# Walking the first softplus stage in tile pairs over two token blocks, with halves in the stage after it

## The chip, the cores and the metric

The kernel runs on one core of a Trainium2 chip. Time is the device time of one execution in microseconds (us). Three runs of the kernel before took 735.72, 737.89 and 739.29 us, so their median is 737.89 us. The engines of the core are called PE (TensorE, matrix products), PEld (its weight loads), DVE (VectorE), ACT (ScalarE), POOL (GpSimd) and SP (SyncE, which issues nearly all DMAs). Each of them works through its own list of instructions in a fixed order.

## The reference, cut to what matters

```python
def reference(**kw):
    attn = _attn_ref(q, k, v, a_re, a_im)        # a decaying linear attention, 2 batches x 8 heads x 768 steps x 48
    x = attn.transpose(0, 2, 1, 3).reshape(1536, 384)
    x = _moe_ref(x, w_in, w_out)                  # h = x @ w_in;  softplus(h) @ w_out;  d_ff = 2048
    return _moe2_ref(x, domain_probs, w1, w2)     # sum over 4 experts: p_e * (relu(x @ w1_e) @ w2_e);  F = 1024

def softplus(h):
    return np.maximum(h, 0.0) + np.log1p(np.exp(-np.abs(h)))
```

The attention state decays by a complex factor per step, `a_re + i a_im`, whose magnitude is capped at 0.999. `w_in` and `w_out` arrive as 64-bit numbers.

## The kernel before, in words

The 1536 tokens are two batches of 768. Attention goes through twelve chunks of 128 tokens in six groups `n` of two chunks (`c` is 0 or 1). The dense part is cut into twelve stages `k` (`ORDER` sets their order). Stages 0 and 1 are the two halves of the 2048 softplus columns for the first batch, 2 to 5 are its four experts, 6 to 11 are the same for the second batch. A stage has eight tiles `f` of 128 columns. Stage 0 goes over its batch in three blocks of 256 tokens, each of which needs the output of one attention group (block 0 needs group 0, and so on); the later stages take two blocks of 384 tokens.

One step (`step`, for a `k`, a block and an `f`) issues the first product `h` (`gemm1`, nine products on PE) and the softplus on ACT (abs, exp, ln) and DVE (tile `e`), then for the step before it the split of the result into a high and a low part `g` (`second`), and for the step three back (`LAG`) the second product `y` (`third`, nine products that add up in PSUM over the tiles `f`). In stage 0 two tiles `f` share one bank and one softplus. When all eight tiles are added, `third` empties PSUM: stage 0 copies to `Y`, stage 1 adds `Y`, splits the sum and writes it over `X`, which the experts read.

Weights of stages 0 and 1 are joined from two 32-bit words into a 32-bit float by three DVE instructions on each half (`join`, lines 70 to 72; tiles `fA`, `fB`), split in a high part on ACT (line 181) and a low part on DVE (line 182), and written to a scratch in memory for the second batch. `A` tiles hold `w_in`, `B` tiles hold `w_out`; there are four pairs per stage. They go round a ring of `NR` = 9 slots. Three weight tiles of stage 1 (n = 2, 3, 4) are put into a pool of their own, `early`, which `swap` later gives up for `X` of the second batch.

For attention, `back(n)` turns a chunk's q and k (`tp`, PE, copied out by ACT), takes scores (`sp`), masks them on DVE (tile `A` on line 684), mixes (`yps`), adds the state (`sps`, then `S` on DVE) and writes `X` (hi by ACT on line 721, lo by DVE on line 722). `logmag`, `s2_units` and `trig` make the decay and the angles: `prefix` sums along a chunk (`pf`, `pl`), and the last row of one chunk is carried into the next through a DMA and an addition on POOL (`carry`, lines 617 to 619, and line 574). An `excursion` loads the other table of ACT's functions (line 97) and loads the first again after it.

The program is recorded unit by unit: `put` and `events` give each unit a due time on a scale where a step is 1, stage 0 begins at 0, and stage 1 at 24. A scheduler behind the recording then sets the order in which each engine's instructions stand.

Of the kernel before, what the change touches and what calls it, by code (L numbers as in the profile page):

```python
# [75 lines left out]
def fast_path(ctx: ExitStack, tc, bad, wsc, qkv, a_re, a_im, w_in, w_out, probs, w1, w2, out):  # L76
# [9 lines left out]
    psum = ctx.enter_context(tc.tile_pool(name="psum", bufs=1, space=PSUM))  # L86
    early_ctx = ExitStack()
    early = early_ctx.enter_context(tc.tile_pool(name="early", bufs=1, side="right"))

# [3 lines left out]
    def behind(ins, earlier):  # L93
        tc.add_manual_dep(ins.ins, earlier.ins.name, NOSYNC, reason="order on one engine")
# [108 lines left out]

    XB = [xa.tile([P, 2, KT, S], F32R, name="X0"), None]
    Yt = [None]
    acc = {}
    home = [ac, None]
    ps_y = [None]
    h_pair = [None]
# [81 lines left out]
    def third(k, blk, f):  # L291
        s = k % 6
        g = g_t.pop((k, blk, f))
        wt = W[k, f // 2 * 2 + 1]
        nf = HALF if k in FAST else FH
        opens, closes = f % nf == 0, f % nf == nf - 1
        b, c0, nch, tok, TB = span(k, blk)
        nj, width = (KT, TB) if s < 2 else (nch, DM)
        if opens:
            yt = psum.tile([P, 2, 512], F32, tag="y", name=f"y{k}_{blk}_{f}", bufs=1)  # L300
            if k == 0:
                ps_y[0] = [yt[:, j // 2, j % 2 * 256:j % 2 * 256 + 256] for j in range(nj)]
            else:
                zt = psum.tile([P, 512], F32, tag="z", name=f"z{k}_{blk}_{f}", bufs=1)
                ps_y[0] = [yt[:, 0, :width], yt[:, 1, :width], zt[:, :width]]
        ys = ps_y[0]
        for j in range(nj):
            for n, (p, q) in enumerate(((0, 0), (0, 1), (1, 0))):
                if s < 2:
                    l_, r_ = wt[:, q, f % 2, j * P:(j + 1) * P], g[p] if k == 0 else g[:, p, :]  # L310
                else:
                    l_, r_ = g[:, p, j * P:(j + 1) * P], wt[:, q, f % 2, :]
                mate = k == 0 and j == 1
                mm = nc.tensor.matmul(ys[j], l_, r_, start=(opens and n == 0 and not mate),  # L314
                                      stop=(closes and n == 2), skip_group_check=k == 0)
                if opens and n == 0:
                    if mate:
                        behind(mm, opened)
                    opened = mm
        if not closes:  # L320
# [6 lines left out]
        elif s == 1:  # L327
            for j in range(KT):
                u = Yt[0][:, j, tok]
                hi, lo = (XB[b][:, i, j, tok] for i in range(2))  # L330
                nc.vector.tensor_tensor(u, ys[j], u, ALU.add)
                nc.scalar.copy(hi, u)
                nc.vector.tensor_tensor(lo, u, hi.bitcast(F32), ALU.subtract)
# [472 lines left out]

    def spare(shape, dt, nm):
        return early.tile(shape, dt, tag=nm, name=nm)

    def lag_out(k):  # L810
        return lambda: (second(*pipe[-1]) if pipe else None)

    for m, k in enumerate(ORDER):
        if k in FAST:
# [23 lines left out]
            continue  # L838
        blks = 3 if k == 0 else 2
        put([lambda k=k, blk=blk, f=f: step(k, blk, f) for blk in range(blks) for f in range(FH)], base[m], base[m + 1])  # L840
        for n in range(8):
            if k == 0:
                pos, gap = -5.2 + 1.6 * n, 0.4
            elif k == 1:
                pos, gap = 8.3 + 2.3 * n, 0.6
            else:
                pos, gap = base[m - 1] + 1 + 1.7 * n, 1.5
            in_early = k == 1 and n in (2, 3, 4)
            if not in_early:
                if len(ring) >= NR:  # L850
                    pos = max(pos, ring[len(ring) - NR] + 0.1)
                ring.append(base[m + 1] - FH + 2 * (n // 2) + 1 + (LAG if n % 2 else 0))
            for i, u in enumerate(weights(k, n, spare if in_early else slot)):
                events.append((pos + gap * i, len(events), u))
    for pos, need, last, k, n in sorted(fast_events):
# [8 lines left out]
    put([lambda: logmag(1, both)] + s2_units(1) + [lambda: s1_load(2), lambda: squares(2, both), lambda: ratio(2, both)]  # L864
        + [excursion(lambda: trig(1), lambda: arctan(2))], -8, 0)
    put(back(1), -0.7, 6.3)
    put([lambda: logmag(2, both)] + s2_units(2) + [excursion(lambda: trig(2))], 1.3, 7.5)
    put(back(2), 8.3, 15.7)

    def swap():  # L870
        early_ctx.close()
        xb = ctx.enter_context(tc.tile_pool(name="xb", bufs=1, side="right"))
        XB[1] = xb.tile([P, 2, KT, S], F32R, name="X1")

    put([swap], base[2] + 3.5, base[2] + 4)
    put([load_probs], base[2] + 1, base[2] + 2)
# [286 lines left out]
```

## Time and profile before

| | |
|---|---|
| median of three runs | 737.89 us (735.72 to 739.29) |
| the profiled execution: span from first to last instruction | 736.2 us |
| PE busy | 703.0 us (95%) |
| DVE busy | 584.7 us (79%) |
| ACT busy | 487.0 us (66%) |
| mean granted TensorE clock | 0.986 of full |

The page gives the span of the profiled execution and not its own device time; the span lies between the fastest run and the median. The strip below cuts the span into 40 slices of 18.4 us, each digit being a busy share in tenths. PE is nearly always busy from the third slice on, DVE is full from the second to the eighth and then eases, and the granted clock is low in the second slice.

```
PE   1688999999999999999999999999999999999996
DVE  6999999955875854648888779988788899988963
ACT  7887886878896856345686666555556667666640
PEclk9699999999999999999999999999999999999998
```

### The profile page before, as it was taken

How to read it: one execution, taken by the hardware profiler on the slowest of the kernel's cores; microseconds unless marked ns; L12 is line 12 of the kernel's file. 1: busy time of each engine (PE TensorE's matmuls, PEld its weight loads, DVE VectorE, ACT ScalarE, POOL GpSimd, SP SyncE). 2: the span in 40 equal slices, each digit the busy share in tenths (PEclk: the TensorE clock that was granted, in tenths of full speed). 3: DMA queues.
4: the chain of work that ended last, by engine and by line, in shares of the span. 5: the costliest groups of instructions: out<-in, count | busy, mean ns of one | idle time of the engine just before them, and what ended most of it. 6: DMA issues, size and time to landing. Idle time of an engine off the chain costs nothing.

```text
span 736.2 us, 13313 instructions
## 1 busy us (share of the span) xinstructions
PE 703.0 (95%) x5171; PEld 676.2 (92%) x5171; DVE 584.7 (79%) x1150; ACT 487.0 (66%) x898; POOL 33.3 (5%) x31
## 2 busy tenths in 40 slices
PE   1688999999999999999999999999999999999996
PEld 0477899999899999999999999999999999999996
DVE  6999999955875854648888779988788899988963
ACT  7887886878896856345686666555556667666640
POOL 1132010000111011000000000000000000000000
PEclk9699999999999999999999999999999999999998
DMA  7655666721211420121022130213454445554501
GB/s 264 195 175 170 230 190 195 228 84 44 75 55 59 122 81 2 59 86 44 23 86 65 29 102 21 87 44 98 128 159 146 137 151 172 151 172 140 172 32 69
DMA packets 36486, 83.56 MB, mean 113 GB/s; under 512 B 4544, under 2 KB 13376, under 8 KB 36416
## 3 DMA queue, kind: packets, MB, share of 16 engines
q1 hardware_dynamic: 36128, 82.35, 35.5%
q8 instruction: 42, 0.69, 0.4%
q10 hardware_dynamic: 288, 0.30, 0.1%
q14 instruction: 28, 0.23, 0.1%
HBM read 73.95 MB, written 8.65 MB: 112 GB/s over the span
## 4 chain that ended last, share of the span: by engine, by line
PE 70%; DVE 10%; DMA 9%; ACT 8%; issue 2%; POOL 1%; SPq 0%; ACTq 0%; POOLq 0%; DVEq 0%
PE y L314 21%; PE h L232 18%; PE z L314 9%; PE px L425 7%; PE pv L425 3%; PE tp L674 2%; DMA rawB<-in_w_dram 2%; DMA chkw<-in_w_in_dram 2%; PE pc L425 2%; PE sp L683 2%; PE yps L699 2%; DMA chki<-in_a_im_dram 1%; PE ya L359 1%; PE sps L710 1%; DVE fA L72 1%
## 5 line engine op out<-in xcount | busy, mean ns | idle before, releaser
L232 PE MATMUL h<-X,A 128*128 128x384 f32 (+1 forms) x936 | 176.1, 329 | 2.5 <-ACT A L181 0.8
L232 PEld LDWEIGHTS h<-X,A 128*128 128x128 f32 x936 | 153.4, 188 | 5.8 <-issue 1.6
L314 PE MATMUL y<-B,g 128*128 128x384 f32 x744 | 150.0, 335 | 0.0
L314 PEld LDWEIGHTS y<-B,g 128*128 128x128 f32 x744 | 131.1, 188 | 0.5 <-issue 0.2
L314 PE MATMUL y<-g,B 128*128 128x384 f32 (+1 forms) x504 | 91.0, 315 | 0.3 <-ACT g L285 0.3
L314 PE MATMUL z<-B,g 128*128 128x384 f32 x372 | 84.7, 334 | 0.0
L314 PEld LDWEIGHTS y<-g,B 128*128 128x128 f32 x504 | 79.3, 189 | 1.9 <-ACT g L285 0.6
L314 PEld LDWEIGHTS z<-B,g 128*128 128x128 f32 x372 | 66.3, 188 | 0.0
L247 ACT ACTIVATE e<-h 128x384 f32<-128x384 f32 (+1 forms) x60 | 30.8, 513 | 37.3 <-PE h L232 36.3
L250 DVE SCALAR_TENSOR_TENSOR e<-h,e 128x384 f32<-128x384 f32 (+1 forms) x60 | 34.9, 581 | 21.0 <-ACT e L103 20.1
L255 DVE SCALAR_TENSOR_TENSOR g<-h,g 128x384 fp32r<-128x384 f32 x32 | 17.7, 554 | 28.2 <-ACT g L254 28.2
L103 ACT ACTIVATE e<-e,b_one 128x384 f32<-128x384 f32 (+1 forms) x60 | 38.2, 637 | 1.3
L103 ACT ACTIVATE e<-e 128x384 f32<-128x384 f32 (+1 forms) x60 | 32.8, 547 | 1.3
L425 PE MATMUL px<-X,sA 128*128 128x384 f32 x144 | 33.7, 339 | 0.0
L425 PE MATMUL px<-XC,sA 128*128 128x384 f32 x144 | 33.0, 337 | 0.1
L314 PE MATMUL z<-g,B 128*128 128x384 f32 x144 | 32.9, 335 | 0.0
L674 PE MATMUL tp<-ident,QK 128*96 128x128 f32 x192 | 27.3, 290 | 5.9 <-DVE QK L665 5.0
L674 PEld LDWEIGHTS tp<-ident,QK 128*96 128x96 f32 x192 | 22.4, 133 | 10.0 <-DVE QK L665 6.2
L254 ACT ACTIVATE g<-h 128x384 fp32r<-128x384 f32 x32 | 15.6, 487 | 21.3 <-PE h L232 21.1
L286 DVE TENSOR_TENSOR g<-e,g 128x384 fp32r<-128x384 f32 x48 | 26.7, 555 | 3.8 <-ACT g L285 3.0
L490 ACT CAST B<-rawB 128x768 fp32r<-128x768 f32 x24 | 20.0, 835 | 14.1 <-DMA rawB<-in_w_dram 7.6
L490 ACT CAST A<-rawA 128x384 fp32r<-128x384 f32 (+1 forms) x48 | 20.3, 457 | 11.6 <-DMA rawA<-in_w_dram 9.2
(204 smaller groups left out, 1424.4 us busy)
## 6 DMA issues: line engine op xcount, KB each, us to landing
rawA<-in_w_dram SPq DMA_DIRECT2D x32, 384.0 KB, 3.0
rawB<-in_w_dram SPq DMA_DIRECT2D x32, 384.0 KB, 3.1
rawA<-in_w_in_dram SPq DMA_DIRECT2D x16, 384.0 KB, 3.7
rawB<-in_w_out_dram SPq DMA_DIRECT2D x16, 384.0 KB, 3.8
chkw<-in_w_in_dram SPq DMA_DIRECT2D x16, 384.0 KB, 3.5
chkw<-in_w_out_dram SPq DMA_DIRECT2D x16, 384.0 KB, 3.3
qk<-in_qkv_dram SPq DMA_DIRECT2D x12, 384.0 KB, 3.3
v<-in_qkv_dram SPq DMA_DIRECT2D x12, 256.0 KB, 3.1
```

The costliest lines, as they stand in the source:

```text
L103: i = nc.scalar.activation(out_, in_, fn, **kw)
L232: nc.tensor.matmul(ps, wt[:, p, kk, o:o + P], XB[b][:, q, kk, tok], start=(n == 0), stop=(n == 3 * KT - 1))
L247: nc.scalar.activation(t, h, AF.Abs)
L250: nc.vector.scalar_tensor_tensor(t, h, 0.0, t, ALU.max, ALU.add)
L254: nc.scalar.activation(g[:, 0, :], h, AF.Relu)
L255: nc.vector.scalar_tensor_tensor(g[:, 1, :], h, 0.0, g[:, 0, :].bitcast(F32), ALU.max, ALU.subtract)
L286: nc.vector.tensor_tensor(g[:, 1, :], t, g[:, 0, :].bitcast(F32), ALU.subtract)
L314: mm = nc.tensor.matmul(ys[j], l_, r_, start=(opens and n == 0 and not mate), stop=(closes and n == 2), skip_group_check=k == 0)
L425: nc.tensor.matmul(ps, lt[:, p, li, :], rhs, start=(start and n == 0), stop=(stop and n == 2), skip_group_check=True)
L490: nc.scalar.copy(hi, src)
L674: nc.tensor.transpose(tp[:96, hh, :], src[:, hf * 4 + hh, :], ident)
L683: nc.tensor.matmul(sp[:, hh, :], kT[:, hh, :], qT[:, hh, :], start=True, stop=True)
```

## The change

Stage 0 no longer walks block by block. The new table `SEQ0` takes tiles f = 0, 1 for blocks 0 and 1, then f = 2, 3 for both, then f = 0 to 3 of block 2, and then each further pair of tiles for all three blocks. Sums of blocks 0 and 1 stand open together in banks `y` and `z`, those of block 2 in two banks of tag `a`. Stage 1 goes in halves of four tiles f: f = 0 to 3 of both blocks, then f = 4 to 7 of both, so that its sums are closed and added to `Y` twice as often. The due times of the weight tiles change (n = 2 to 7 of stage 0 and all of stage 1 come later), those of the attention groups 1 and 2 become earlier, and the pool `early` is gone, since `X` of the second batch now has its own place from the start.

```diff
+SEQ0 = ([(blk, 2 * j + i) for j in range(2) for blk in range(2) for i in range(2)] + [(2, f) for f in range(4)]
+        + [(blk, 2 * j + i) for j in range(2, 4) for blk in range(3) for i in range(2)])
...
-    early_ctx = ExitStack()
-    early = early_ctx.enter_context(tc.tile_pool(name="early", bufs=1, side="right"))
+    xb = ctx.enter_context(tc.tile_pool(name="xb", bufs=1, side="right"))
...
-        nf = HALF if k in FAST else FH
+        nf = HALF if k in FAST or k == 1 else FH
...
+            if k == 0 and blk == 2:
+                ya, yb = (psum.tile([P, 512], F32, tag="a", name=f"y{nm}{k}_{blk}", bufs=3) for nm in "ab")
+                ps_y[blk] = [ya[:, lower], ya[:, upper], yb[:, lower]]
+            elif k or blk == 0:
+                yt = psum.tile([P, 2, 512], F32, tag="y", name=f"y{k}_{blk}_{f}", bufs=1)
                 zt = psum.tile([P, 512], F32, tag="z", name=f"z{k}_{blk}_{f}", bufs=1)
...
                 nc.vector.tensor_tensor(u, ys[j], u, ALU.add)
+                if f < FH - 1:
+                    continue
                 nc.scalar.copy(hi, u)
...
-        put([lambda k=k, blk=blk, f=f: step(k, blk, f) for blk in range(blks) for f in range(FH)], base[m], base[m + 1])
+        seq = SEQ0 if k == 0 else [(blk, f + i) for f in ((0, HALF) if k == 1 else (0,)) for blk in range(2)
+                                   for i in range(HALF if k == 1 else FH)]
+        put([lambda k=k, blk=blk, f=f: step(k, blk, f) for blk, f in seq], base[m], base[m + 1])
...
-                pos, gap = -5.2 + 1.6 * n, 0.4
+                pos, gap = (-5.2, -4.2, 1.0, 2.2, 8.2, 10.0, 12.5, 14.5)[n], 0.4
             elif k == 1:
-                pos, gap = 8.3 + 2.3 * n, 0.6
+                pos, gap = 16.5 + (2.4 * n if n < 4 else 2.6 + 1.6 * n), 0.6
...
-    put(back(1), -0.7, 6.3)
-    put([lambda: logmag(2, both)] + s2_units(2) + [excursion(lambda: trig(2))], 1.3, 7.5)
-    put(back(2), 8.3, 15.7)
+    put(back(1), -2.5, 1.9)
+    put([lambda: logmag(2, both)] + s2_units(2) + [excursion(lambda: trig(2))], 0.2, 4.2)
+    put(back(2), 4.4, 7.9)
```

The order of the instructions changes with it. In the rows below a name carries its place in front of a buffer number: `h0_0_2` is `h` of stage 0, block 0, tiles 2 and 3; `fB1_3_0` is half 0 of the fourth `B` tile of stage 1; `g10_2_7` is the low part `g` of stage 0, block 2, tiles 6 and 7; lines differ by up to ten between the two files.

PE, where the first product of stage 0 begins and the turn of chunk 0 of attention group 1 (`tp1_0`) follows. Before:

```order
L232 MATMUL h0_0_0_548<-X0_119,A0_0_351 128x256 x2
L232 MATMUL h0_0_2_677<-X0_119,A0_1_501 128x256 x2
L232 MATMUL h0_0_0_548<-X0_119,A0_0_351 128x256 x16
L232 MATMUL h0_0_2_677<-X0_119,A0_1_501 128x256 x16
L674 MATMUL tp1_0_0_566<-ident_84,QK1_0_536 96x128 x4
```

Now:

```order
L234 MATMUL h0_0_0_639<-X0_119,A0_0_361 128x256 x18
L684 MATMUL tp1_0_0_526<-ident_84,QK1_0_518 96x128 x4
L684 MATMUL tp1_0_0_533<-ident_84,QK1_0_518 96x128 x4
L684 MATMUL tp1_0_1_540<-ident_84,QK1_0_518 96x128 x4
L684 MATMUL tp1_0_1_547<-ident_84,QK1_0_518 96x128 x4
```

Eighteen products of tiles 2 and 3 that stood ahead of the turn now stand behind attention group 1.

DVE, at the end of stage 0, where the last `e` and `g` of stage 0 and the first `e` of stage 1 stand among the joins of stage 1. Before:

```order
L250 SCALAR_TENSOR_TENSOR e0_2_7_1746<-h0_2_6_1702,e0_2_7_1746 128x512
L182 TENSOR_TENSOR A1_3_1725<-fA1_3_0_1730,A1_3_1725 128x384
L72 SCALAR_TENSOR_TENSOR fA1_3_1_1760<-rawA1_3_1_1728,fA1_3_1_1760 128x384
L276 TENSOR_TENSOR g10_2_7_1783<-e0_2_7_1746,g00_2_7_1782 128x512
L70 TENSOR_SCALAR fB1_3_0_1827<-rawB1_3_0_1796 128x384
L182 TENSOR_TENSOR A1_3_1725<-fA1_3_1_1760,A1_3_1725 128x384
L71 SCALAR_TENSOR_TENSOR fB1_3_0_1827<-rawB1_3_0_1796,fB1_3_0_1827 128x384
L250 SCALAR_TENSOR_TENSOR e1_0_0_1777<-h1_0_0_1767,e1_0_0_1777 128x384
```

Now:

```order
L252 SCALAR_TENSOR_TENSOR e0_2_7_1676<-h0_2_6_1633,e0_2_7_1676 128x512
L72 TENSOR_SCALAR fB1_3_0_1982<-rawB1_3_0_1976 128x384
L183 TENSOR_TENSOR A1_3_1896<-fA1_3_1_1938,A1_3_1896 128x384
L73 SCALAR_TENSOR_TENSOR fB1_3_0_1982<-rawB1_3_0_1976,fB1_3_0_1982 128x384
L278 TENSOR_TENSOR g10_2_7_1711<-e0_2_7_1676,g00_2_7_1710 128x512
L252 SCALAR_TENSOR_TENSOR e1_0_0_1705<-h1_0_0_1695,e1_0_0_1705 128x384
```

The joins of stage 1 stand as far along at this place as they did; three instructions of the last pair that stood behind `g10_2_7` stand ahead of it, and one more, the split of the first weight tile of stage 2, stands further up (`A2_0<-rawA2_0`, 128x768).

ACT, at the end of stage 1, where the front of attention group 3 (`im3`, `t23`, `hl3`) stands among the last softplus tiles. Before:

```order
L103 ACTIVATE e1_1_6_2243<-e1_1_6_2243 128x384
L285 CAST g1_1_5_2248<-e1_1_5_2207 128x384
L103 ACTIVATE e1_1_6_2243<-e1_1_6_2243,b_one_102 128x384
L580 ACTIVATE hl3_0_0_2261<-im3_2153 128x384
L181 CAST B2_3_2299<-rawB2_3_2300 128x768
```

Now:

```order
L104 ACTIVATE e1_1_6_2242<-e1_1_6_2242 128x384
L287 CAST g1_1_5_2247<-e1_1_5_2205 128x384
L104 ACTIVATE e1_1_6_2242<-e1_1_6_2242,b_one_102 128x384
L342 CAST X0_119<-Y0_1656 128x384 x3
L590 ACTIVATE hl3_0_0_2271<-im3_2152 128x384
```

The three casts of `X` for block 0, which stood in the middle of stage 1, now stand directly ahead of the first `hl3` of attention group 3.

## Rows read from the trace of the kernel before

**Rows 1.** The page, its span and first line: busy us, share, instructions.
```profile
span 736.2 us, 13313 instructions
...
PE 703.0 (95%) x5171; PEld 676.2 (92%) x5171; DVE 584.7 (79%) x1150; ACT 487.0 (66%) x898; POOL 33.3 (5%) x31
```
**Rows 2.** Windows: stretch, length, busy of PE, PEld, DVE, ACT, POOL, clock, DMA.
```profile
30.00:139.30 109.30, 103.54 (x1223) 92.25 (x1223) 104.11 (x193) 87.00 (x157) 15.14 (x10) 0.97 0.62 196
56.66:92.21 35.55, 33.23 (x417) 29.00 (x418) 33.72 (x63) 28.83 (x53) 5.93 (x4) 1.00 0.60 196
92.21:140.10 47.89, 47.89 (x521) 45.93 (x520) 46.23 (x93) 35.51 (x69) 2.44 (x1) 1.00 0.63 197
140.10:178.96 38.86, 38.86 (x228) 38.65 (x228) 25.07 (x46) 33.12 (x67) 0.00 (x0) 1.00 0.32 100
```
**Rows 3.** Timeline of DVE: start us, length us, work; idle before it in brackets.
```profile
65.22 2.13 DVE L72 SCALAR_TENSOR_TENSOR fA<-rawA,fA 128x384 int32<-128x384 int32 x1
...
138.69 0.69 DVE L276 TENSOR_TENSOR g<-e,g 128x512 fp32r<-128x512 f32 x1 [0.19 <-ACT g L275]
139.30 0.35 DVE L70 TENSOR_SCALAR fB<-rawB 128x384 int32<-128x384 int32 x1
139.57 0.55 DVE L182 TENSOR_TENSOR A<-fA,A 128x384 fp32r<-128x384 f32 x1
140.04 0.55 DVE L71 SCALAR_TENSOR_TENSOR fB<-rawB,fB 128x384 int32<-128x384 int32 x1
...
144.16 0.96 DVE L182 TENSOR_TENSOR A<-rawA,A 128x768 fp32r<-128x768 f32 x1
```
**Rows 4.** Timeline of PE at three places of stage 0.
```profile
51.36 4.09 PE L232 MATMUL h<-X,A 128*128 128x256 f32 x32 [0.26 <-DVE X L722]
56.66 0.53 PE L674 MATMUL tp<-ident,QK 128*96 128x128 f32 x3 [1.21 <-DVE QK L665]
...
140.10 1.23 PE L314 MATMUL y<-g,B 128*128 128x256 f32 x9
```
**Rows 5.** The chain that ended last, 93 to 120 us: start, length, work.
```profile
94.06 1.76 PE tp L674 x16
...
97.94 0.89 PE sp L683 x8
...
102.68 1.02 PE sps L710 x48
...
113.89 1.95 PE yps L699 x64
...
118.18 1.08 PE h L232 x9
```
**Rows 6.** Timeline of the last row carried between the chunks of attention group 2.
```profile
63.81 0.91 PE L593 MATMUL pf<-im,trik 128*128 128x384 f32 x2
...
70.54 0.53 DVE L601 SCALAR_TENSOR_TENSOR im<-im,pf 128x384 f32<-128x384 f32 x1
...
77.47 1.05 POOL L574 TENSOR_TENSOR im<-rows,im 1x384 f32<-1x384 f32 x1 [6.58 <-DMA rows<-tail]
...
78.57 0.91 PE L593 MATMUL pf<-im,trik 128*128 128x384 f32 x2 [0.41 <-POOL im L574]
```
**Rows 7.** Timeline at the change of blocks in stage 1.
```profile
168.84 1.02 DVE L331 TENSOR_TENSOR Y<-y,Y 128x384 f32<-128x384 f32 x2 [0.18 <-PE y L314]
...
169.16 1.73 PE L232 MATMUL h<-X,A 128*128 128x384 f32 x9
```
**Rows 8.** Timeline: casts of X in stage 1, and PE waiting for `hl3`.
```profile
169.57 0.91 ACT L332 CAST X<-Y 128x384 fp32r<-128x384 f32 x2
...
195.47 0.44 PE L586 MATMUL pf<-hl,tri_r 128*128 128x384 f32 x1 [0.45 <-ACT hl L580]
```
**Rows 9.** Windows around the fall of PE's clock; columns as in Rows 2.
```profile
24.00:28.00 4.00, 1.03 (x5) 0.99 (x6) 3.91 (x9) 3.92 (x8) 0.00 (x0) 0.74 0.46 150
28.00:36.00 8.00, 7.22 (x23) 4.34 (x22) 7.20 (x13) 7.19 (x12) 2.18 (x2) 0.50 0.76 246
```

More of the change, by code (lines that the diff above doesn't have):

```diff
@@ L202, in weights @@
         return [load2, lambda: conv(0), lambda: conv(1)]
-    XB = [xa.tile([P, 2, KT, S], F32R, name="X0"), None]
+    XB = [pool.tile([P, 2, KT, S], F32R, name=f"X{i}") for i, pool in enumerate((xa, xb))]
     Yt = [None]
@@ L207, in fast_path @@
     home = [ac, None]
-    ps_y = [None]
+    ps_y = {}
+    opener = {}
     h_pair = [None]
@@ L299, in third @@
         if opens:
[L300 to L303, printed above, removed]
-                zt = psum.tile([P, 512], F32, tag="z", name=f"z{k}_{blk}_{f}", bufs=1)
-                ps_y[0] = [yt[:, 0, :width], yt[:, 1, :width], zt[:, :width]]
-        ys = ps_y[0]
+            lower, upper = slice(0, 256), slice(256, 512)
+            if k == 0 and blk == 2:
[3 more added lines that the diff above has]
+                yt = psum.tile([P, 2, 512], F32, tag="y", name=f"y{k}_{blk}_{f}", bufs=1)
+                zt = psum.tile([P, 512], F32, tag="z", name=f"z{k}_{blk}_{f}", bufs=1)
+                if k == 0:
+                    for i, third_ in enumerate((lower, upper)):
+                        ps_y[i] = [yt[:, i, lower], yt[:, i, upper], zt[:, third_]]
+                else:
+                    ps_y[blk] = [yt[:, 0, :width], yt[:, 1, :width], zt[:, :width]]
+        ys = ps_y[blk]
         for j in range(nj):
@@ L312, in third @@
                     l_, r_ = g[:, p, j * P:(j + 1) * P], wt[:, q, f % 2, :]
-                mate = k == 0 and j == 1
+                mate = {(0, 1): (0, 0), (1, 1): (1, 0), (2, 1): (2, 0), (1, 2): (0, 2)}.get((blk, j)) if k == 0 else None
                 mm = nc.tensor.matmul(ys[j], l_, r_, start=(opens and n == 0 and not mate),
@@ L317, in third @@
                     if mate:
-                        behind(mm, opened)
-                    opened = mm
+                        behind(mm, opener[mate])
+                    opener[blk, j] = mm
         if not closes:
@@ L805, in slot @@
         return wp.tile(shape, dt, tag="w", name=nm, bufs=NR)
-    def spare(shape, dt, nm):
-        return early.tile(shape, dt, tag=nm, name=nm)
     def lag_out(k):
@@ L838, in fast_path @@
             continue
-        blks = 3 if k == 0 else 2
-        put([lambda k=k, blk=blk, f=f: step(k, blk, f) for blk in range(blks) for f in range(FH)], base[m], base[m + 1])
+        seq = SEQ0 if k == 0 else [(blk, f + i) for f in ((0, HALF) if k == 1 else (0,)) for blk in range(2)
+                                   for i in range(HALF if k == 1 else FH)]
+        put([lambda k=k, blk=blk, f=f: step(k, blk, f) for blk, f in seq], base[m], base[m + 1])
         for n in range(8):
             if k == 0:
-                pos, gap = -5.2 + 1.6 * n, 0.4
+                pos, gap = (-5.2, -4.2, 1.0, 2.2, 8.2, 10.0, 12.5, 14.5)[n], 0.4
             elif k == 1:
-                pos, gap = 8.3 + 2.3 * n, 0.6
+                pos, gap = 16.5 + (2.4 * n if n < 4 else 2.6 + 1.6 * n), 0.6
             else:
                 pos, gap = base[m - 1] + 1 + 1.7 * n, 1.5
[L848 to L853, printed above, removed]
+            if len(ring) >= NR:
+                pos = max(pos, max(ring[:len(ring) - NR + 1]) + 0.1)
+            ring.append(base[m] + max(i for i, (blk, f) in enumerate(seq) if f == n // 2 * 2 + 1) + (LAG if n % 2 else 0))
+            for i, u in enumerate(weights(k, n, slot)):
                 events.append((pos + gap * i, len(events), u))
@@ L864, in fast_path @@
     put([lambda: logmag(1, both)] + s2_units(1) + [lambda: s1_load(2), lambda: squares(2, both), lambda: ratio(2, both)]
-        + [excursion(lambda: trig(1), lambda: arctan(2))], -8, 0)
-    put(back(1), -0.7, 6.3)
-    put([lambda: logmag(2, both)] + s2_units(2) + [excursion(lambda: trig(2))], 1.3, 7.5)
-    put(back(2), 8.3, 15.7)
[L870 to L875, printed above, removed]
+        + [excursion(lambda: trig(1), lambda: arctan(2))], -8, -2.6)
+    put(back(1), -2.5, 1.9)
+    put([lambda: logmag(2, both)] + s2_units(2) + [excursion(lambda: trig(2))], 0.2, 4.2)
+    put(back(2), 4.4, 7.9)
     put([load_probs], base[2] + 1, base[2] + 2)
```

## The prediction, made before the changed kernel ran

> **What bounds the kernel now.** I read the page's first part, then the windows, then PE's and DVE's timelines around the places that the change touches. PE is busy for 703.0 of the 736.2 us of the span [rows 1], so a change can only gain where PE stands still or is held up. The windows show where: from 92 us on PE is busy without a break (47.89 of 47.89 us to 140 us, 38.86 of 38.86 us to 179 us), while between 56.66 and 92.21 us 2.3 us are plainly idle [rows 2]. In those same stretches DVE is the engine that is full: from 30 to 139.3 us it works 104.11 of 109.30 us, and it eases only when stage 0 is over (25.07 of 38.86 us) [rows 2]. So up to 140 us two engines stand close together, and the reader should see which one sets the end of stage 0. PE begins the last `y` of stage 0 at 140.10 us [rows 4]; DVE has finished the `g` that it needs at 138.69 + 0.69 = 139.4 us [rows 3]. The slack is under 1 us. A gain must therefore move both.
>
> How much PE loses in stage 0 follows from unit prices. A turn of one chunk takes 1.76 us, its scores 2 x 0.89 = 1.78, its mix 1.95, its state 1.02, nine products over 256 columns 1.08 us [rows 5]; a prefix takes about 0.9 us [rows 6], and nine products over 384 columns about 1.6 us (1.73 with the overlap of the next) [rows 7]. Between the first turn of group 1 (56.66 us) and the last `y` (140.10 us) stand group 1 at 2 x 6.51 = 13.0 us; group 2 at 13.0 less one state plus four prefixes, 15.6; 20 `h` at 21.6; two `h` of stage 1 at 3.2; 22 `y` at 23.8. That is 77.2 us of 83.4, so 6.2 us are lost, and no rearrangement of this stretch can win more than that from PE.
>
> **The change part by part.** *The joins.* Their due times go back, yet the order of DVE's list shows how little leaves the full stretch. Up to the last `g` of stage 0 the new list holds everything that the old one held and four instructions more: a first and a second join instruction, one split, and the wide split for stage 2. One instruction begins 0.27 us after a short join and 0.47 us after a long one or a split (139.30, 139.57, 140.04), the wide one holds DVE about 0.9 us (0.96 with its overlap) [rows 3]: 0.27 + 0.47 + 0.47 + 0.9 = 2.1 us more. What the change moves back is the first half of this work only, from before the attention groups to behind them. If DVE idles as before (5.2 us from 30 us on [rows 2]), the last `g` comes 2.1 us later. If it never idled it would come 3.1 us earlier; if it idled twice as long, 7.3 us later.
>
> *The first step and attention.* Ahead of group 1's turn PE now has 18 products instead of 36 (32 of these took 4.09 us, the turn then waited 1.21 us [rows 4]). The `QK` that the turn waits for has five DVE instructions less ahead of it, 4 x 0.47 + 0.27 = 2.15 us; so the turn begins between 54.5 and 56.66 us. I take 55.5, since in the new list the masks of chunk 0 stand ahead of the second weight tile's splits and wait there for the scores, which gives half of it back. PE then has 77.2 us plus the 18 products left over, 2.2: it would reach the last `y` at 134.9 us without any wait, at 141.1 with the old 6.2 us of waits. Groups 1 and 2 now run with little beside them, so waits for a mask, a copy out of PSUM or a `QK` are bare; their sum is somewhere between 2 and 11 us, which gives 136.9 to 145.9. DVE's sum and PE's agree on a small loss, +2.1 and +1.0. I take +2.0 us for stage 0, with ends -3.1 (DVE's floor, above PE's) and +5.8.
>
> *The products, the banks, the pool.* The number of products is the same. Two open sums in `y` and `z` and two banks of `a` cost nothing as long as nobody else wants these banks; the mixes of group 1, which use `z`, stand before the first `y` of its sum except for one product, and only the low-sum checks share `a` with block 2. The pool `early` goes; `swap` issued nothing on an engine. Bounds: 0 to +1 us, taken 0.
>
> *Halves in stage 1.* Six more additions on DVE, about 0.5 us each (two in 1.02 us [rows 7]), 3 us in a stretch with 13.8 us of DVE idle [rows 2]. Each change of sums makes PE wait until `Y` has been added, but a step's `h` of 1.6 us stands between: at the one change of blocks in stage 1 that the trace has, the two additions began 0.18 us after `y` and took 1.02 us while PE ran an `h` of 1.73 us [rows 7]. There are three such places instead of one, so I cost them at 0; without the cover each would cost up to 1.2 us, +2.4 in all.
>
> *From stage 1 to stage 2.* With halves, `X` of block 0 is final only four tiles before stage 2 and not twelve. Its three casts on ACT (two took 0.91 us, so 1.3 us [rows 8]) now stand ahead of the first `hl3`. PE already waits 0.45 us for the second `hl3` [rows 8], so this chain has no slack, and it leads to group 3's turn. In the new order four more products (0.7 us) cover that turn. Between 0 and +1.8 us; I take +0.8, near the row of the wait plus what the products leave over.
>
> The sum is +2.8 us on the profiled span of 736.2, or 739.0. That span lies 1.7 us below the median of the runs shown and 0.5 above the fastest, and what lies around the span isn't shown; I put the result 1 us above the sum, at 740.0 us.
>
> **The rivals.**
> *A, the forecast:* both sums hold, 738.5 to 742 us. Chance 0.45.
> *B, faster:* the joins set back let groups 1 and 2 run through with DVE nearly never idle. For it speaks that the plain idle time of PE lies where DVE is full. Against it speaks the list: its floor is -3.1 us, and lower only if an overlap with POOL goes too (a join that takes 0.55 us took 2.13 beside POOL, 1.6 us [rows 3]). With the transition hidden the time is 736.2 - 3.1 - 1.6 = 731.5 us at the least, and 735 where half of it is had. Chance 0.15.
> *C, slower, the carried row:* in the new order the second prefix of group 2 stands behind two products of `h0_1_0`, with all further dense work behind it. In the old trace the way from one prefix to the next took 78.57 - 63.81 = 14.8 us, with 6.7 us until the wrapped row and 6.9 us from there to POOL [rows 6]. The new list has only some 5.9 us of PE work there, the first prefix included, and with the waits I count about 8.7. If the carry takes over 8.7 us PE stops; at 14.8 us it stops for 6.1, of which 1.5 are in my waits. 740.0 + 4.6 = 744.6, range 743 to 747.5. Against it: DVE's list now has fewer joins ahead of the wrap. Chance 0.15.
> *D, slower, PE's clock:* in the old trace PE was busy 1.03 of 4 us between 24 and 28 us, and then the granted clock was 0.50 for all of the next 8 us, which is the lower level, 1.2 GHz [rows 9]; later gaps of 1.21 us left it at 1.00 [rows 2, 4]. The new gap before group 1's turn is about 55.5 - 53 = 2.5 us. If the clock fell there, a turn, scores, mix and state (6.5 us) would take up to twice as long: +3 to +6.5, or 743 to 746.5 us. The Trainium skill, page "TensorE: Matmul & The Clock Gate", section "Why this matters for your kernels", advises against such gaps between bursts because the clock then returns to half; the trace agrees for the larger gap, and no row shows one of 2.5 us. Chance 0.06.
> *E, the change doesn't do what it says:* the joins end where they ended, DVE idles a little less, and nothing moves: 735.5 to 738.5. Chance 0.19.
>
> A second rule bears on the new list, where the last softplus tile ahead of group 2 is cut by two table loads. The Trainium skill, page "ScalarE: Activation LUTs", section "What ACT_TABLE_LOAD costs", puts 1.38 us of drain on each load beside 1.28 us for itself, which would make the wait for that `g` 2.8 us longer and the time 742.8 us at most. The sum above leaves it out.
>
> **How the numbers follow.** About 0.5%, 3.7 us, is what a measurement of this kernel can tell from no change, so faster means under 734.2 and slower over 741.6 us. B gives 0.12 to faster and 0.03 to the same. E is the same, 0.19. Of A 0.35 are the same and 0.10 slower. C and D are slower, 0.21. That is 0.12 faster, 0.57 the same, 0.31 slower. The range 733.5 to 746.0 leaves out the lower part of B and the tails of C and D, less than 2 in 10.
>
> **What would show it.** DVE still full to the end of stage 0, and the last `g` of stage 0 at about 141 us; the last `y` about 142; the first turn of group 1 near 55.5 us. More waits of PE between 56 and 105 us with shorter dense work beside them, and no new wait at the three changes of sums in stage 1. `hl3` about 1 us later against stage 1's end. I am wrong if the last `y` of stage 0 begins before 138 us (then the joins did leave the full stretch, or DVE's waits were shorter than any that I count), if PE stops over 3 us ahead of the second prefix of group 2 (C), or if the clock falls after 50 us (D). DVE's overlaps with POOL will fall on other instructions; I can't place them.

## The result and the profile after

The changed kernel takes 745.60 us (median of 4 runs, 743.55 to 748.0), the kernel before 738.02 us on the same chip (4 runs, 735.72 to 739.29): a ratio of 1.0108, 95% interval 1.0088 to 1.0128, so slower by some 8 us. The profiled execution is the longest of the four; its span of 746.2 us lies 1.9 to 4.4 us above the others (741.8 to 744.3).

The page of the changed kernel, to be read against [rows 1]: the same number of products on PE, six additions more on DVE.

```profile
span 746.2 us, 13328 instructions
...
PE 705.6 (95%) x5171; PEld 679.1 (91%) x5171; DVE 586.5 (79%) x1156; ACT 488.9 (66%) x898; POOL 31.2 (4%) x31
```

Busy time answers nothing here: 10.0 us of span, of which 2.6 are PE's. So I cut the program at four places that both traces have: the first turn of group 1, the first turn of group 2, the last nine `y` of stage 0, and the first turn of group 3. First the kernel before, then the changed one (windows; columns as in [rows 2]).

```profile
56.66:93.89 37.23, 34.91 (x431) 30.67 (x432) 35.40 (x65) 30.51 (x56) 5.93 (x4) 1.00 0.57 187
93.89:142.79 48.90, 48.90 (x524) 46.94 (x523) 47.21 (x97) 36.30 (x71) 2.44 (x1) 1.00 0.66 208
142.79:209.26 66.47, 65.68 (x372) 63.70 (x372) 41.96 (x73) 58.98 (x109) 2.63 (x2) 1.00 0.25 76
```

```profile
54.88:91.25 36.37, 31.36 (x389) 27.70 (x389) 30.89 (x57) 25.24 (x45) 5.11 (x4) 0.91 0.58 183
91.25:149.90 58.65, 56.80 (x584) 54.43 (x585) 55.04 (x107) 43.21 (x82) 2.59 (x1) 1.00 0.66 201
149.90:221.13 71.23, 67.67 (x377) 65.84 (x376) 44.91 (x80) 59.36 (x110) 2.00 (x2) 0.98 0.21 65
```

The reader is to look at the counts behind PE. The changed kernel comes to group 2 at 91.25 us, 2.6 us earlier, but has issued 42 matmuls less on the way from group 1, and 60 more are left for the second stretch, which grows by 9.75 us. Everything up to the last `y` of stage 0 adds up to 149.90 - 142.79 = 7.1 us. The third stretch adds 4.8 us in this execution; the profiles of the experiments below show that most of that isn't there as a rule.

The waits behind it, from PE's timeline of the changed kernel (start, length, work, idle before it and what ended it), to be read against [rows 4] and [rows 6]:

```profile
54.88 3.55 PE L684 MATMUL tp<-ident,QK 128*96 128x128 f32 x16 [2.78 <-DVE QK L675]
...
67.27 0.81 PE L603 MATMUL pf<-im,trik 128*128 128x384 f32 x2
...
75.09 1.47 PE L603 MATMUL pf<-im,trik 128*128 128x384 f32 x2 [2.13 <-POOL im L584]
...
91.25 2.02 PE L684 MATMUL tp<-ident,QK 128*96 128x128 f32 x16 [1.12 <-DVE QK L675]
...
105.70 0.86 PE L709 MATMUL yps<-A,v 128*32 128x128 f32 x24 [1.08 <-DVE A L694]
...
116.09 0.74 PE L322 MATMUL ya<-g,B 128*128 128x256 f32 x4 [0.58 <-DVE g L278]
...
147.26 0.87 PE L322 MATMUL ya<-g,B 128*128 128x256 f32 x6
...
149.90 0.87 PE L322 MATMUL ya<-g,B 128*128 128x256 f32 x6
...
153.04 2.62 PE L234 MATMUL h<-X,A 128*128 128x384 f32 x9 [1.92 <-DVE e L252]
```

In the kernel before, the turns of groups 1 and 2 waited 1.21 us and not at all, the prefix 0.41 us, and PE had no break in the second stretch. Behind the three longest of these waits the granted clock falls to its lower level, 1.2 GHz, which the kernel before doesn't show between 36 us and the last microseconds of its span. Windows of the changed kernel (clock is the third number from the end):

```profile
51.90:54.88 2.98, 0.21 (x2) 0.03 (x2) 2.98 (x5) 2.98 (x7) 0.00 (x0) 0.99 0.92 267
54.88:58.29 3.41, 3.40 (x16) 3.05 (x16) 3.41 (x5) 2.83 (x6) 0.00 (x0) 0.51 0.67 219
75.09:78.50 3.41, 3.41 (x11) 2.45 (x12) 3.41 (x9) 1.72 (x3) 0.00 (x0) 0.53 0.74 222
153.04:156.45 3.41, 3.41 (x13) 3.41 (x14) 1.63 (x3) 2.98 (x9) 0.00 (x0) 0.61 0.59 173
```

DVE's part, to be read against [rows 3]: the last `g` of stage 0 comes at 146.64 us (138.69 before). From 30 us to 147.25 DVE is idle for 12.3 us (5.2 up to 139.30 before); counted by the waits that its timeline shows up to the last `g`, it is 11.6 and 4.1 us. Two of its waits will matter below:

```profile
87.44 0.69 DVE L278 TENSOR_TENSOR g<-e,g 128x512 fp32r<-128x512 f32 x1 [2.46 <-ACT g L277]
...
146.64 0.69 DVE L278 TENSOR_TENSOR g<-e,g 128x512 fp32r<-128x512 f32 x1
...
150.63 0.36 DVE L72 TENSOR_SCALAR fB<-rawB 128x384 int32<-128x384 int32 x1 [2.36 <-DMA moe_weights<-fA]
```

So the traces leave four candidates: PE's clock, DVE's idle time, the squeeze of attention into fewer steps, and the new order of the steps; the halves of stage 1 and the late join at 150.63 us are two more.

### The profile page after: what moved, and what is told of

It reads as the page before. It is cut to its first block, busy times and chain, and to the rows that moved or that the text cites. A ratio compares the mean times of both kernels' runs of the same rounds, so it can differ in the third digit from the quotient of the medians.

```text
span 746.2 us, 13328 instructions
## 1 busy us (share of the span) xinstructions
PE 705.6 (95%) x5171; PEld 679.1 (91%) x5171; DVE 586.5 (79%) x1156; ACT 488.9 (66%) x898; POOL 31.2 (4%) x31
## 4 chain that ended last, share of the span: by engine, by line
PE 70%; DMA 10%; DVE 9%; ACT 8%; issue 2%; SPq 1%; POOL 1%; ACTq 0%; DVEq 0%; POOLq 0%
PE y L322 20%; PE h L234 17%; PE z L322 10%; PE px L435 7%; PE pv L435 4%; DMA chkw<-in_w_in_dram 3%; PE pc L435 3%; PE tp L684 2%; PE sp L693 2%; PE yps L709 1%; DMA moe_weights<-fA 1%; DMA chki<-in_a_im_dram 1%; ACT L98 1%; DMA rawB<-in_w_out_dram 1%; DMA rows<-tail 1%
## 5 line engine op out<-in xcount | busy, mean ns | idle before, releaser
L322 PE MATMUL y<-g,B 128*128 128x384 f32 (+1 forms) x384 | 75.6, 327 | 0.9 <-ACT g L287 0.9
L322 PEld LDWEIGHTS y<-g,B 128*128 128x128 f32 x384 | 65.0, 191 | 1.9 <-ACT g L287 1.2
L252 DVE SCALAR_TENSOR_TENSOR e<-h,e 128x384 f32<-128x384 f32 (+1 forms) x60 | 34.8, 580 | 17.3 <-ACT e L104 16.2
L322 PE MATMUL z<-g,B 128*128 128x384 f32 (+1 forms) x192 | 41.9, 322 | 0.0
L684 PE MATMUL tp<-ident,QK 128*96 128x128 f32 x192 | 29.2, 299 | 8.5 <-DVE QK L675 7.4
L322 PEld LDWEIGHTS z<-g,B 128*128 128x128 f32 x192 | 32.9, 189 | 0.0
L256 ACT ACTIVATE g<-h 128x384 fp32r<-128x384 f32 x32 | 15.6, 489 | 20.6 <-PE h L234 20.3
```

The lines of the kernel that those rows point to most:

```text
L252: nc.vector.scalar_tensor_tensor(t, h, 0.0, t, ALU.max, ALU.add)
L256: nc.scalar.activation(g[:, 0, :], h, AF.Relu)
L684: nc.tensor.transpose(tp[:96, hh, :], src[:, hf * 4 + hh, :], ident)
```

## The experiments

All times are medians; the kernel before, run beside them on each chip, had 736.6 to 736.9 us, and each ratio is to that. The 745.60 us of the changed kernel stand beside 738.02 us, so the ratios compare better than the times. G, W, P, J, S and the others are named in the expectations.

**Products that nobody reads, in the three waits (e1, e6).**

```diff
+ for _ in range(22):   # ahead of the first turn of group 1; 16 ahead of pf(2,1), 14 ahead of h(1,0,3)
+     nc.tensor.matmul(tp[:, 0, :], ident, tri, start=True, stop=True)
```

> The changed kernel with 52 products more on PE that nobody reads (128x128 fp32, about 0.11 us each by the turns' x16 in 1.76 us): 22 ahead of the first turn of group 1, 16 ahead of group 2's second prefix, 14 ahead of h(1,0,3), each where PE stood idle 2.78, 2.13 and 1.92 us. Theory G (each of these waits also drops PE's clock to half for 3.41 us, at about 1.7 us each): the clock stays at its upper level behind 36 us, the turn takes 1.8 instead of 3.55 us, the last sums of stage 0 come 3 to 3.5 us earlier (about 144) and the end about 5 us earlier (740 to 741.5). Rival W (only the waits count, DVE sets the pace and hides a slower PE): 745 to 746.5, last sums at 147.

752.72 us, ratio 1.0215 (1.0195 to 1.0235): 7 us slower than the changed kernel and outside both forecasts. I had mis-sized them; each is two matmuls in the trace and takes over 0.22 us (44 matmuls in 5.18 us), so this is some 12 us of work where 6.8 us of waits were to be filled. The timeline of e1 shows it ahead of the turn:

```profile
48.57 5.18 PE L692 MATMUL tp<-tri,ident 128*128 128x128 f32 x44
54.29 1.96 PE L694 MATMUL tp<-ident,QK 128*96 128x128 f32 x16 [0.54 <-DVE QK L682]
```

The clock did stay up and the turn took 1.96 instead of 3.55 us, but the last `y` comes at 153.25 us (149.90 in the changed kernel). So e6 repeats it with 10, 8 and 7.

> The changed kernel with PE kept busy again, with 10, 8 and 7 products in place of 22, 16 and 14 (at the 0.22 us each that these took: 2.2, 1.8 and 1.6 us). Theory G (the falls of the clock cost some 1.7 us each): no fall behind 36 us, last g of stage 0 by 144 and 741 to 742.5. Rival P (VectorE's idle time sets the end of stage 0, and PE at half clock hides behind it): the clock stays up and the time stays at 744 to 747, last g at 146 to 147.

751.55 us, ratio 1.0197 (1.0177 to 1.0217). This too lies outside both forecasts. One fall of the clock is left (at 74.5 us, behind a wait of 1.86 us that ended at 73.72). The last `y` begins at 151.01 us: the first two fillings, 4 us put into waits of 4.9 us, gave nothing back, nor did the clock. The third meets a wait that is not there as a rule (e8 below) and counts in full. Some 3 us more arise behind 520 us, far from the edit, where the profile shows 1.2 us of PE's waits (0.2 in the changed kernel); what they are stays open, and the two runs bear only on the clock up to 150 us. There they speak against G, but don't refute it, since the fillings cost PE time themselves.

**The halves of stage 1, taken out (e2) and alone (e3).**

```diff
- nf = HALF if k in FAST or k == 1 else FH
+ nf = HALF if k in FAST else FH             # e2, with the sequence of stage 1 in one run
```

> The changed kernel with stage 1 again in one run of eight f tiles a block. Theory H (the halves with the casts of X late cost 2 to 4 us behind stage 0): 742 to 743.5. Rival (the halves cost nothing, what is late in stage 1 comes from the joins moved back): 745 to 746, the same wait of about 2 us of h(1,0,3) around 153 us.

> The kernel before with stage 1 alone in halves of four f tiles. Theory H: 740 to 742, all of it behind 157 us. Rival: within 0.7 us of 738, with the first turn of group 3 at most 1 us later than 209.3.

e2: 744.37 us, 1.0103 (1.0086 to 1.012). e3: 736.58 us, 0.9998 (0.9985 to 1.001). The halves cost nothing that the times show: e3 lies with the rival, and e2, between its two forecasts, gains 0.4 us by the ratios, within the noise. In e3 the way from the last `y` to group 3's turn is 67.35 us (66.47 before), 0.9 longer; in e2, without halves, it is 67.71 us.

**Attention's due times alone, on the kernel before (e4).**

```diff
- put(back(1), -0.7, 6.3)
+ put(back(1), -2.5, 1.9)
- put(back(2), 8.3, 15.7)
+ put(back(2), 4.4, 7.9)      # and the units ahead of each, as in the changed kernel
```

> The kernel before (its order of blocks, its joins, its early weights) with only the due times of attention of the changed kernel: groups 1 and 2 squeezed into 4.4 and 3.5 steps. Theory G (bare attention on PE makes gaps that the clock answers): a wait of 2 us or more ahead of group 1's turn or group 2's second prefix, clock down behind it, last sums of stage 0 at 143 to 147, time 741 to 746. Rival S (the order of the sums over two blocks and the joins moved back cost it, not the squeeze): 737 to 739.

742.02 us, 1.0078 (1.0057 to 1.0098): 5 us, on the side of G by its time. But the first turn waits only 0.26 us, the second prefix 0.59; the wait that G names is at group 2's turn, and ahead of it PE waits for a weight that isn't joined and split yet:

```profile
84.61 0.39 PE L232 MATMUL h<-X,A 128*128 128x256 f32 x1 [1.78 <-ACT A L181]
86.73 3.53 PE L674 MATMUL tp<-ident,QK 128*96 128x128 f32 x16 [1.73 <-DVE QK L665]
```

**The joins of stage 0 due as before (e5).**

```diff
- pos, gap = (-5.2, -4.2, 1.0, 2.2, 8.2, 10.0, 12.5, 14.5)[n], 0.4
+ pos, gap = -5.2 + 1.6 * n, 0.4
```

> The changed kernel with the joins of stage 0's weights due as in the kernel before (from -5.2 in steps of 1.6); sequence, banks, attention's due times and stage 1 as changed. VectorE sets the pace up to the last g of stage 0 in both kernels (138.69 us before, 146.64 after; idle from 30 us 4.1 and 11.6 us). Theory J (joins moved back leave VectorE idle beside the squeezed attention, and the same work comes due later): idle falls to about 7, last g near 143.5, time about 741.5 to 743. Rival S (the squeeze of attention alone makes the idle time, 7.1 us where only its due times were changed, and the rest is the sequence): idle stays above 10, 744 to 746; or, if joins now stand ahead of QK in VectorE's list, the first turn of group 1 comes at 57 to 59 us.

745.53 us, 1.0119 (1.0094 to 1.0144), idle time of DVE 12.1 us to the last `g` (the waits of its timeline from 30 us on, as the 11.6 and 4.1 us above), the first turn at 55.30 us behind the same 2.78 us. Theory J falls: that the joins were moved back costs nothing in the order that the changed kernel has. In e5 the second pair of weights is due at -2.0 and -0.4, exactly as in e11 and e12 below, so joining it early gains nothing by itself either.

**The second prefix of group 2 behind more products (e7); the last join of stage 1 later (e8).**

```diff
- put([lambda: logmag(2, both)] + s2_units(2) + [excursion(lambda: trig(2))], 0.2, 4.2)
+ put([lambda: logmag(2, both)] + u2[:3], 0.2, 2.48)                  # e7, u2 = s2_units(2)
+ put(u2[3:] + [excursion(lambda: trig(2))], 3.1, 4.3)
```

```diff
- events.append((pos + gap * i, len(events), u))
+ events.append((pos + gap * i + (1.2 if (k, n, i) == (1, 7, 2) else 0.0), len(events), u))   # e8
```

> The changed kernel with group 2's second prefix and what follows it due later (from 3.1 on in place of 2.5), so that 16 products h and nine of the sums stand ahead of it on PE. Theory G: the wait of 2.1 us at 75 us and the fall of the clock behind it go, 3 to 4 us less, 741 to 742.5. Rival P: VectorE does not wait there, the end of stage 0 moves by less than 1 us (744.5 to 746.5); it is slower than that if group 2's sines then come late (QK of group 2, 91.25 us for its first turn).

> The changed kernel with one join due 1.2 steps later, the second half of the last weights of stage 1, which held VectorE 2.36 us at 150.63 us until the store of the join before it had landed (its buffer). Theory W (this wait stops g, then h(1,0,3) by 1.9 us, and drops the clock for 3.4 us): the wait and the fall behind 153 us go, 2 to 3.5 us less, 741.5 to 743. Rival (PE has work to catch up with later, or the next join waits the same): 744.5 to 746.

e7: 746.06 us, 1.0121 (1.0098 to 1.0144). The wait of 2.13 us is gone, and two others have come for it:

```profile
76.64 3.44 PE L234 MATMUL h<-X,A 128*128 128x256 f32 x16 [3.23 <-DVE X L732]
...
92.73 3.25 PE L684 MATMUL tp<-ident,QK 128*96 128x128 f32 x16 [2.46 <-DVE QK L675]
```

The products set ahead of the prefix need group 1's `X` themselves, and the last `y` comes at 153.09 us, later than the 149.90 us of the changed kernel. e8: 745.71 us, 1.0116 (1.0096 to 1.0137). The wait of `h(1,0,3)` shrinks from 1.92 to 0.72 us, the clock stays up there, and the time doesn't move. In the profiles of e2, e5, e9, e11 and e12 the way from the last `y` to group 3's turn takes 67.5 to 67.7 us without this edit, against the 71.23 us shown above: so that wait is not there as a rule, and not part of the 8 us. What these profiles have over the 66.47 us of the kernel before is 1.0 to 1.2 us.

**8 us less on DVE (e9), 8 us less on PE (e10).** e9 leaves the three lowest bits out of stage 0's weights, e10 the products of the low part of X in stage 0.

```diff
- nc.vector.scalar_tensor_tensor(f, raw[:, :, 0], 29, f, ...)   # e9: not for stage 0
- for (p, q) in ((0, 0), (1, 0), (0, 1)):                       # e10: without (0, 1) in stage 0
```

> The changed kernel without the third instruction of each join of stage 0's weights (it leaves out their three lowest bits): 16 instructions of 0.47 to 0.55 us less on VectorE, some 8 us, 11 or so of them behind the first turn of group 1; PE as changed. Theory P (VectorE sets the pace of stage 0; what the change costs is its idle time): last g of stage 0 5 to 7 us earlier (140 to 142), time 738 to 741. Rival G/PE (PE's waits and clock set it): VectorE's idle time grows by what is taken out, last g less than 2 us earlier, 743 to 746.

> The changed kernel without the 72 products of stage 0's h with the low part of X (0.108 us each, 7.7 us of PE); VectorE as changed. Theory P: last g of stage 0 less than 2 us earlier, time 743 to 746 (the one gain is what follows the last g). Rival PE: 5 to 8 us earlier, 738 to 741.

e9: 744.15 us, 1.0101 (1.0083 to 1.0119). e10: 740.11 us, 1.005 (1.0035 to 1.0065). In e9 DVE does 8 us less and the kernel gains 1.4 us (0.5 by the ratios); DVE's idle time to the last `g` grows from 11.6 to 17.3 us, and this `g` comes 1.5 us later than in the changed kernel. In e10 PE does 7.7 us less and the kernel gains 5.5 us (4.3 by the ratios); the last `g` comes 9.0 us earlier. First e9, then e10:

```profile
148.10 0.68 DVE L279 TENSOR_TENSOR g<-e,g 128x512 fp32r<-128x512 f32 x1
```

```profile
137.66 0.68 DVE L279 TENSOR_TENSOR g<-e,g 128x512 fp32r<-128x512 f32 x1
```

Theory P, which I had formed from DVE's idle time, falls: less work on DVE only makes it wait longer, and the end of stage 0 moves with PE's list. (e10 also frees `h` from waiting for the low part of `X`, and no run took work off ACT.) e9 bounds the price of the clock as well, by windows of its two first stretches and of the two that follow its waits of 2.30 and 2.21 us:

```profile
54.99:90.00 35.01, 28.92 (x389) 25.43 (x389) 28.54 (x54) 25.41 (x46) 6.33 (x4) 1.00 0.62 197
90.00:150.58 60.58, 57.41 (x583) 54.60 (x584) 52.45 (x99) 41.70 (x79) 2.59 (x1) 1.00 0.55 175
```

```profile
54.99:58.40 3.41, 3.41 (x28) 2.94 (x29) 3.38 (x5) 3.41 (x8) 0.00 (x0) 1.00 0.43 122
75.86:79.27 3.41, 3.41 (x21) 2.88 (x22) 1.59 (x3) 2.46 (x6) 0.00 (x0) 1.00 0.95 297
```

With the clock up and the same 389 matmuls, the first stretch is 1.4 us shorter than in the changed kernel (36.37), PE's busy time 2.4 us less and its idle time 1.1 us more. So by this run the two falls of the clock in stage 0 are worth 1.4 us there at most: of the 2.4 us that PE saves by running faster it spends 1.1 waiting. At the last `y` nothing of the gain is left (150.58 us, against 149.90).

**Another order of the steps (e11, e12).** Both run four tiles of block 0 and then four of block 1, where the changed kernel takes two and two; the second pair of weights is joined early for that. Sums over two blocks, banks and halves stay. e11 also gives attention more room; e12 puts attention's due times back to those of the changed kernel.

```diff
- SEQ0 = ([(blk, 2 * j + i) for j in range(2) for blk in range(2) for i in range(2)] + [(2, f) for f in range(4)] + ...
+ SEQ0 = ([(blk, f) for blk in range(2) for f in range(4)] + [(blk, f) for blk in range(2) for f in (4, 5)]
+         + [(2, f) for f in range(6)] + [(blk, f) for blk in range(3) for f in (6, 7)])
- (-5.2, -4.2, 1.0, 2.2, 8.2, 10.0, 12.5, 14.5)[n]
+ (-5.2, -3.6, -2.0, -0.4, 3.4, 5.4, 11.0, 13.0)[n]
- put(back(1), -2.5, 1.9)     # e11 alone: -2.0 to 3.5, group 2 from 6.3 to 11.9
```

> The changed kernel's idea with attention given room: stage 0 as block 0 f 0 to 3, block 1 f 0 to 3, both f 4 and 5, then block 2 f 0 to 5, then all three f 6 and 7; sums over two blocks, banks and halves as changed; group 1 due from -2.0 to 3.5 (-2.5 to 1.9 in the changed kernel, -0.7 to 6.3 before), group 2 from 6.3 to 11.9 (4.4 to 7.9; 8.3 to 15.7 before), joins of the second pair due from -2.0. Theory S (attention squeezed beside too little other work makes VectorE's idle time, 11.6 us up to the last g against 4.1): idle 5 to 8, last g 140 to 143, time 738 to 741.5. Rival Q (the sums over two blocks, their banks or the joins moved back are what costs): idle stays above 10, 743 to 747.

> The sequence and the joins of e11 (four tiles of block 0, then four of block 1, before the others), with attention's due times put back to those of the changed kernel (group 1 from -2.5 to 1.9, group 2 from 4.4 to 7.9). What counts by theory S is how many products of stage 0 PE has done when group 2's turn begins (174 before, at 93.89 us; 114 changed, at 91.25; 148 in e11, at 89.08; 93 with attention's times alone, at 86.73). If the squeeze alone makes the loss: 85 to 100 products at 85 to 88 us, 742 to 744, as in e4 (742.0). If the order of the steps is a second cause by itself, this order takes it away and 740 to 742 follows. If the squeeze is no cause and e11 was helped by its order alone: 737 to 739.

e11: 737.60 us, 1.0014 (1.0004 to 1.0025). e12: 738.49 us, 1.0026 (1.0013 to 1.0038). With attention squeezed exactly as in the changed kernel, e12 loses 1.9 us in place of 8, by its time the third of the outcomes that it allowed for: most of the loss comes from the order of the steps. e12 differs from e5 in that order and in the due times of the last four joins alone, and those lie between the ones of e5 and of the changed kernel, two kernels that take the same time (ratios 1.0119 and 1.0108). The squeeze by itself is not without a price: it costs 5 us in the order of the kernel before (e4). In e11 DVE is idle for 9.7 us to the last `g`, outside the 5 to 8 that theory S named, and yet its loss is about 1 us. PE's timeline of e12, against that of the changed kernel above:

```profile
49.57 3.48 PE L234 MATMUL h<-X,A 128*128 128x256 f32 x25 [0.20 <-ACT X L731]
53.28 1.58 PE L234 MATMUL h<-X,A 128*128 128x256 f32 x11 [0.24 <-DVE A L183]
55.11 2.11 PE L684 MATMUL tp<-ident,QK 128*96 128x128 f32 x16 [0.25 <-DVE QK L675]
...
73.34 0.91 PE L603 MATMUL pf<-im,trik 128*128 128x384 f32 x2 [0.51 <-POOL im L584]
...
85.36 1.51 PE L684 MATMUL tp<-ident,QK 128*96 128x128 f32 x12 [0.70 <-DVE QK L675]
```

The first turn begins within 0.25 us of that of the changed kernel, but 36 products are done by then and not 18: they fill the wait of 2.78 us, since they need block 0 and two weights and nothing of group 1. The second prefix comes 1.75 us earlier, and group 2's turn 5.9.

Why the way from the prefix to the turn shrinks too, from 16.2 to 12.0 us, is on ACT. The changed kernel, where a softplus tile of block 1 (from 80.20 us on) stands ahead of group 2's sines:

```profile
81.77 0.72 ACT L104 ACTIVATE e<-e,b_one 128x512 f32<-128x512 f32 x1
82.51 1.28 ACT L98 ACT_TABLE_LOAD   x1
83.80 0.94 ACT L104 ACTIVATE re<-re,b_hpi 128x768 f32<-128x768 f32 x1
84.65 0.83 ACT L104 ACTIVATE im<-im 128x768 f32<-128x768 f32 x1
85.49 1.28 ACT L98 ACT_TABLE_LOAD   x1
86.79 0.62 ACT L277 CAST g<-e 128x512 fp32r<-128x512 f32 x1
```

and e12, where the sines follow the prefix at once, since the first of the two table loads already stood at 60.88 us:

```profile
77.29 0.85 ACT L645 ACTIVATE re<-im 128x768 f32<-128x768 f32 x1
78.17 0.94 ACT L104 ACTIVATE re<-re,b_hpi 128x768 f32<-128x768 f32 x1
79.01 0.83 ACT L104 ACTIVATE im<-im 128x768 f32<-128x768 f32 x1
79.86 1.28 ACT L98 ACT_TABLE_LOAD   x1
```

This shorter way is not what saves the time, though: in e11, which loses least, it is 17.2 us (71.89 to 89.08).

One table gives the sum. Products are those over 256 columns, 435 in all, counted in PE's list (the expectation of e12 counted one to four more); "net" is a stretch less 0.12 us for each product in it (nine take 1.08 us [rows 5]), so it holds attention, waits and a slow clock. To the second stretch all the rest of the 435 are counted, the last nine `y` at its end with them. In the last column the changed kernel's time was taken beside 738.0 us for the kernel before, the others beside 736.6 to 736.9.

| kernel | products ahead of group 1's turn | first stretch us | products in it | net | second stretch us | net | last `y` at | median |
|---|---|---|---|---|---|---|---|---|
| before | 36 | 37.23 | 135 | 21.0 | 48.90 | 17.2 | 142.79 | 736.7 |
| changed | 18 | 36.37 | 92 | 25.3 | 58.65 | 19.7 | 149.90 | 745.6 |
| e4 attention early | 36 | 31.10 | 56 | 24.4 | 60.82 | 19.7 | 147.55 | 742.0 |
| e5 joins back | 18 | 36.04 | 92 | 25.0 | 59.28 | 20.3 | 150.62 | 745.5 |
| e9 less DVE | 18 | 35.01 | 92 | 24.0 | 60.58 | 21.6 | 150.58 | 744.2 |
| e11 | 36 | 34.37 | 110 | 21.2 | 53.21 | 18.5 | 142.29 | 737.6 |
| e12 | 36 | 30.25 | 73 | 21.5 | 58.02 | 18.9 | 143.38 | 738.5 |

Attention of the first stretch costs 21 us where PE's list has products that can run, and 24 to 25 where it hasn't: in the changed kernel because the next steps need group 1 itself, in e4 because the old order asks for the third pair of weights before it is joined. These reasons are read from the order of the list and from the waits shown; no run changed either of them alone. The changed kernel loses 4.3 us there, 2.4 in the second stretch (its waits of 1.08 and 0.58 us for a mask and a `g` are among them), and 0.4 ahead of the first turn (18 products undone are 2.2 us, for 1.8 us earlier): the 7.1 us. By another cut of the same two stretches, 4.5 us are idle time of PE (6.9 us, against 2.3 before) and 2.2 us are longer work of PE, with two stretches at the slow clock in it; these and the 0.4 are again 7.1.

## Where the prediction was right and where it went wrong

The time lies inside the range of 733.5 to 746.0 us, but by luck: slower had a chance of 0.31, the likeliest case, 740.0 us, was 5.6 us short, and the upper end of the range came from the rivals C and D, neither of which, by e7 and e9, set the time. Step by step:

- *DVE and PE set the end of stage 0 together, slack under 1 us.* The row was read rightly, but the conclusion was wrong: e9 and e10 show that the end moves with PE's list, not with DVE's. DVE's work up to there grew by 1.0 us (127.35 to 128.32 us) and not by 2.1, and the same idle time (5.2 us) was no premise to build on: it became 12.3 us because DVE waited.
- *First turn of group 1 at 55.5 us.* 54.88, with 18 products ahead of it as counted and a wait of 2.78 us ("about 2.5").
- *PE: 77.2 us + 2.2 us + 6.2 us of waits, 2 to 11 us.* This is the step that failed. The `y` at 140.10 us, which was in fact the last batch of nine but one, came at 147.26: 147.26 - 54.88 - 79.4 = 13.0 us lost, where 6.2 were taken and 11 was the bound. It forecast 141.1 because it asked how many products are left over at group 1's turn only and kept the old waits. At group 2's turn the list has 110 products done and not 171: 61 x 0.12 = 7.3 us left over, for 2.6 us earlier, and 2.4 us more are lost behind it. The 110 and the 171 stood in the order of PE's list before anything ran.
- *Banks and pool 0.* Borne out within its bound of 1 us by e11, which keeps them and loses about 1 us in all.
- *Halves 0, from stage 1 to 2 +0.8.* The halves cost nothing in the time (e3, ratio 0.9998); the leg behind them is 0.9 us longer there, near the +0.8, but not by the wait that was forecast. PE doesn't wait for `hl3` in e3 or in the changed kernel; it waits 0.37 and 0.36 us for a cast of `X`, and in the changed kernel 0.91 us for a late `g` of stage 1. The `g` is as late in e2, which has no halves. At the changes of sums PE doesn't wait, as forecast. The 0.18 us of [rows 7] was misread: it is DVE's idle time ahead of the additions (0.20 us now), which begin within 0.1 us of the end of the last `y` in both kernels.
- *1 us from the span to the time.* Too little: in the four runs of the changed kernel the time is 1.7 to 1.8 us longer than the span, about as far as the span of 736.2 us lies below the 737.89 us of the kernel before.
- *Rival C.* PE stopped 2.13 us ahead of the second prefix, under the 3 us set for it, although the carry took 75.09 - 67.27 = 7.8 us, less than the 8.7 us of its threshold: PE had 5.7 us of work and waits there, since the waits counted into the 8.7 were not there. e7 took the stop away, got two others and gained nothing.
- *Rival D, 0.06.* Its mechanism took place, and at three waits, not one, so this sign of being wrong came true; its price of 3 to 6.5 us did not. By e9 the two falls in stage 0 are worth 1.4 us at most, beside the longer waits ahead of them. The rule cited from the Trainium skill, "TensorE: Matmul & The Clock Gate", section "Why this matters for your kernels", says that the clock goes back to half behind gaps between bursts, and means longer ones than these. The trace agrees on the half (0.51, 0.53 and 0.61 in the windows behind three waits), not on the gaps: here it fell behind 1.92 to 2.78 us, and in e9 it stayed up behind 2.30 us.
- *The second rule, from the Trainium skill, "ScalarE: Activation LUTs", section "What ACT_TABLE_LOAD costs".* The rows above disagree with a drain on top: the instruction ahead ends at 82.49, the load starts at 82.51, and the next one starts 1.29 us later. What the excursion costs is the 4.3 us from the first load to the cast of `g`, for which DVE waits 2.46 us at 87.44 us.

Still open: what made e6 some 3 us later behind 520 us; where e12 loses the 1.9 us that are left; and whether the order of e12 would do as well with other joins, for it needs the second pair early. The early pair without that order, in e5, gained nothing.

## What to carry to other kernels

Where a chain of short dependent steps is run beside dense products on an in-order engine, count in its list how many of those products stand ahead of each link of the chain and can run without it; in this kernel what wasn't done by then was added at the end at its full price, 7.3 us for 61 products. An engine's idle time says that it waits, not that it sets the pace: take work off it and off its neighbour, one at a time, before a theory is built on it. And a step that needs the chain's own result is no cover for the chain.

## What the hardware showed besides

The granted clock fell behind waits of PE of 1.73 us (e4, 0.4 us behind another wait, of 1.78 us), 1.86 (e6), 1.92, 2.13 and 2.78 us (changed kernel), and stood at its lower level for 3.41 us; it stayed up behind 2.30 and 2.21 us in e9 and behind 1.66 us in e5. The length of the wait alone doesn't decide it. And the falls left little mark on the time, as far as one profiled execution of each kernel tells: e7 has three of them between 50 us and the last microseconds, e8 two, e5 one, and the medians of all three lie within 0.6 us of each other.
